# Fewer weight chunks split during attention, a new VectorE order within a period, one reciprocal for seven tiles, six warming matmuls

## The chip, the cores and the metric

The kernel runs on one core of a Trainium2 chip. The metric is the device time of one execution in microseconds (us), and less is better. The engines of the core work side by side and meet at semaphores: TensorE (PE in the profile, its weight loads PEld), VectorE (DVE), ScalarE (ACT), GpSimd (POOL) and SyncE (SP), which only issues DMAs.

## The reference

Causal attention over 24 heads (batch 2, 12 heads, 448 positions, head size 64), then two feed-forward blocks, each of two layers:

```python
scores = scale * np.matmul(q, k.transpose(0, 1, 3, 2))
scores = np.where(mask, -1000000000.0, scores)
scores = scores - np.max(scores, axis=-1, keepdims=True)
attn = np.exp(scores)
attn = attn / (np.sum(attn, axis=-1, keepdims=True) + 1e-09)
x = np.matmul(attn, v)                         # -> (896, 768)
h = x @ w_in;  g = np.maximum(h, 0.0) + alpha * np.minimum(h, 0.0);  x = g @ w_out
h = x @ w_in2; g = (h + 1)**2 / 4 between -1 and 1, h above, 0 below; out = g @ w_out2
```

The weights are drawn in 64-bit floats; the host only lays them out, and the kernel reads them as pairs of 32-bit words.

## The kernel before

**Attention.** The heads are worked in 12 pairs (`NP` = 12). A period n does the scores of pair n, the transposes of pair n-1 and the product with v of pair n-2, so three pairs are in flight. Period 0 is written apart (`first_pair`), periods 12 and 13 empty the pipeline. The program's order is the order in the code (`manual_schedule`): each engine runs its own instructions strictly one after the other.

The scores of a pair are four row blocks i = 0 to 3. Blocks 0, 1 and 2 are 128, 256 and 384 wide and have one tile for each head of the pair; block 3 is 448 wide and holds both heads in one tile. That makes seven tiles. In a period

- TensorE does `scores` of pair n (L347 for block 3, L353 for blocks 2, 1, 0), `attnv` of pair n-2 (L435), and the transposes of pair n-1 (`transp`: L407 for block 3, L415 for block 2, L425 for blocks 1 and 0).
- VectorE does `low` (L364): mask, scale and row minimum for the seven tiles. It then copies transposed tiles out of PSUM: block 3 (L511), the first tile of block 2 (L512), block 0 (L515). ScalarE copies the other tile of block 2 (L513) and block 1 (L514).
- ScalarE does `expo` (L373) on the seven tiles.
- VectorE then adds 1e-9 to the row sums and takes the reciprocal (`inverse`, L380 and L381), and GpSimd multiplies the tiles by it (L386). This is done twice in a period: first for the three tiles of blocks 3 and 2, at the period's end for the four tiles of blocks 1 and 0.
- `evac_x` brings the finished output of pair n-2 out of PSUM as a high and a low part: ScalarE rounds (`high`, L220), VectorE subtracts (`low`, L223).

Seven PSUM banks go round over the scores and the transposes (12 uses a period), the eighth holds the output of `attnv`. A tile of the next scores waits until the use of its bank seven places earlier has been read. Block 2's second tile takes the bank of the L511 copy, the tiles of block 1 those of L512 and L513, the tiles of block 0 those of L514 and L515.

**Weights.** 80 chunks of 64-bit weights are loaded, turned into a 32-bit value and split into a rounded high part and a rest, so that TensorE can multiply in its fast mode. A chunk takes: a magnitude on ScalarE (L112), `clamp` (L128), `low_bits` (L134), `high_bits` (L140), `last_bits` (L146) followed by the rounding on ScalarE (L149), and `rest` (L152). Chunks 0, 1 and 2 are prepared by the generator `prime` during attention. It is stepped once in each period from 1 on, ahead of `high`, so that one step is one or two of these operations, and clamp and rest run on GpSimd. Chunks 3 and on are split by VectorE and ScalarE while TensorE multiplies with the chunks before (`run_layer`).

**The four layers.** 2304 matmuls of 448 columns (`products`, L255). A chunk of the first layer is 36 of them. The first ones, with the first chunk, run already in periods 12 and 13 (`early_tiles`, `FILL`).

**The start.** `warm_up` issues three matmuls of 512 columns on a tile of zeros while the first inputs are loaded.

## Time and profile before

| | us |
|---|---|
| runs shown, three: lowest, median, highest | 561.75, 571.18, 571.21 |
| the profiled execution: its own time | 561.79 |
| its span, first to last instruction | 560.0 |
| attention: up to the last `attnv` and the unbroken row of layer matmuls | 92.75 |
| the four layers after that | 467.25 |

The page names each engine's busy time and share of the span. The view by stretches gives busy times between chosen moments; the timeline gives instructions in order of time, neighbours of one line merged, with the idle time ahead of them and what ended it. The two slower runs lie 1.7% above the profiled execution.

### The profile page before, as it was taken

What the parts mean: (1) busy time and instruction counts of PE and PEld (TensorE: products, weight loads), DVE (VectorE), ACT (ScalarE), POOL (GpSimd) and SP (SyncE); (2) the same over time, 40 slices, a digit from 0 to 9 for tenths busy, and PEclk for the clock granted to TensorE, in tenths of its full rate; (3) what the DMA queues carried; (4) which work ended last, traced back from release to release, by engine and by line L of the source; (5) the groups of instructions that cost most, each with busy time, mean ns of one, the idle gap of its engine ahead of it and who ended that gap; (6) DMA issues with size and microseconds to landing.
All of it is one profiled execution on the core that took longest, in us unless ns stands there. A gap on an engine that the chain in (4) does not pass through costs nothing.

```text
span 560.0 us, 8112 instructions
## 1 busy us (share of the span) xinstructions
PE 552.2 (99%) x2883; PEld 486.4 (87%) x2883; DVE 420.0 (75%) x812; ACT 236.6 (42%) x485; POOL 147.3 (26%) x170
## 2 busy tenths in 40 slices
PE   8999999999999999999999999999999999999997
PEld 4666567999999999999999999999999999999996
DVE  5888884888898988765666678898888867555740
ACT  6877772333333323332323345555554423222220
POOL 5776861333333331000000013333333300000000
PEclk9999999999999999999999999999999999999999
DMA  7543520333232224433423432333322244343421
GB/s 261 163 128 88 167 73 1 114 110 102 95 99 103 77 74 132 133 82 107 128 100 112 169 90 100 111 114 113 114 95 75 77 140 150 114 141 117 146 70 35
DMA packets 24040, 61.88 MB, mean 110 GB/s; under 512 B 3392, under 2 KB 12352, under 8 KB 24000
## 3 DMA queue, kind: packets, MB, share of 16 engines
q1 hardware_dynamic: 21984, 59.76, 33.7%
q10 hardware_dynamic: 2016, 1.61, 0.8%
q8 instruction: 23, 0.38, 0.3%
q14 instruction: 17, 0.14, 0.1%
HBM read 58.60 MB, written 2.75 MB: 110 GB/s over the span
## 4 chain that ended last, share of the span: by engine, by line
PE 86%; DVE 7%; ACT 4%; issue 1%; DMA 1%; POOL 0%; ACTq 0%; DVEq 0%; POOLq 0%
PE ps L255 83%; ACT pexp L373 3%; DVE pexp L364 2%; PE o_ps L435 1%; DVE pt L511 1%; DVE x L223 1%; ACT x L220 1%; DVE pt L512 1%; PE ps L353 1%; DMA qk_raw<-qk 1%; DVE pt L515 1%; DVE stat L380 0%; DVE w_f L146 0%; PE ps L415 0%; PE ps L407 0%
## 5 line engine op out<-in xcount | busy, mean ns | idle before, releaser
L255 PE MATMUL ps<-x,w_split 128*128 128x448 f32 x1152 | 234.5, 365 | 0.0
L255 PE MATMUL ps<-g,w_split 128*128 128x448 f32 x1152 | 233.8, 365 | 0.0
L255 PEld LDWEIGHTS ps<-g,w_split 128*128 128x128 f32 x1152 | 216.3, 188 | 17.1
L255 PEld LDWEIGHTS ps<-x,w_split 128*128 128x128 f32 x1152 | 216.1, 188 | 17.2
L184 POOL TENSOR_TENSOR g<-act_g,g 128x448 fp32r<-128x448 f32 x64 | 85.5, 1337 | 272.5 <-ACT g L183 272.4
L149 ACT CAST w_split<-w_f 128x512 fp32r<-128x512 f32 (+1 forms) x80 | 56.6, 707 | 124.7 <-DVE w_f L146 82.0
L152 DVE TENSOR_TENSOR w_split<-w_f,w_split 128x512 fp32r<-128x512 f32 (+1 forms) x77 | 63.1, 820 | 52.3 <-ACT w_split L149 52.3
L183 ACT CAST g<-act_g 128x448 fp32r<-128x448 f32 x64 | 36.2, 565 | 81.5 <-DVE act_g L196 71.6
L140 DVE SCALAR_TENSOR_TENSOR w_f<-w_raw,w_f 128x512 uint32<-128x512 uint32 (+1 forms) x80 | 63.4, 793 | 1.4
L146 DVE SCALAR_TENSOR_TENSOR w_f<-w_raw,w_f 128x512 uint32<-128x512 uint32 (+1 forms) x80 | 63.4, 793 | 1.4
L128 DVE TENSOR_SCALAR w_f<-w_f 128x512 f32<-128x512 f32 (+1 forms) x77 | 56.4, 733 | 8.7 <-ACT w_f L112 8.6
L112 ACT ACTIVATE w_f<-w_raw 128x512 f32<-128x512 f32 (+1 forms) x80 | 61.2, 765 | 0.6 <-DMA w_raw<-w 0.6
L386 POOL TENSOR_SCALAR pexp<-pexp,stat 128x256 f32<-128x256 f32 (+3 forms) x84 | 44.7, 552 | 24.4 <-DVE stat L381 14.4
L373 ACT ACTIVATE pexp<-pexp,stat 128x128 f32<-128x128 f32 (+3 forms) x84 | 43.7, 521 | 16.7 <-DVE stat L364 16.7
L134 DVE TENSOR_SCALAR w_f<-w_f 128x512 uint32<-128x512 uint32 (+1 forms) x80 | 38.4, 480 | 1.4
L208 ACT ACTIVATE act_t<-act_t,half 128x448 f32<-128x448 f32 x32 | 21.5, 671 | 37.4 <-DVE act_t L207 37.4
L364 DVE CUSTOM_DVE_ANT_0 pexp<-ps,mask 128x128 f32<-128x128 f32 (+3 forms) x84 | 32.5, 447 | 4.7 <-PE ps L353 4.3
L353 PEld LDWEIGHTS ps<-qk_raw 64*128 64x128 f32 x144 | 17.0, 196 | 15.8 <-issue 4.9
L353 PE MATMUL ps<-qk_raw 64*128 64x256 f32 (+2 forms) x144 | 25.9, 424 | 1.8 <-ACT pt L513 1.1
L233 DVE COPY o_sb<-ps 128x224 f32<-128x224 f32 x12 | 4.7, 391 | 29.9 <-ACT o_sb L233 29.9
L191 DVE TENSOR_SCALAR act_t<-ps,alpha_sb 128x448 f32<-128x448 f32 x32 | 21.8, 681 | 3.8 <-PE ps L255 3.7
L435 PE MATMUL o_ps<-pt,v 128*64 128x448 f32 (+3 forms) x192 | 23.4, 386 | 0.0
(42 smaller groups left out, 254.7 us busy)
## 6 DMA issues: line engine op xcount, KB each, us to landing
w_raw<-w SPq DMA_DIRECT2D x32, 768.0 KB, 4.3
w_raw<-w SPq DMA_DIRECT2D x48, 512.0 KB, 3.6
qk_raw<-qk SPq DMA_DIRECT2D x11, 448.0 KB, 3.8
out<-o_sb SPq DMA_DIRECT2D x12, 112.0 KB, 1.7
out<-o_sb ACTq DMA_DIRECT2D x12, 112.0 KB, 1.7
v<-v SPq DMA_DIRECT2D x12, 56.0 KB, 3.9
v<-v SPq DMA_DIRECT2D x12, 48.0 KB, 3.4
v<-v SPq DMA_DIRECT2D x12, 40.0 KB, 2.8
```

The source lines that it names most:

```text
L112: nc.scalar.activation(out=f32(w), in_=f32(hi), func=AF.Abs)
L128: side.tensor_scalar(out=f32(w), in0=f32(w), scalar1=HI_MIN, scalar2=HI_MAX, op0=ALU.max, op1=ALU.min)
L140: nc.vector.scalar_tensor_tensor(out=w, in0=hi, scalar=0xC0000000, in1=w, op0=ALU.bitwise_and, op1=ALU.bitwise_or)
L146: nc.vector.scalar_tensor_tensor(out=w, in0=lo, scalar=29, in1=w, op0=ALU.logical_shift_right, op1=ALU.bitwise_or)
L149: nc.scalar.copy(s[:, 0, :n], f32(w))
L152: side.tensor_sub(s[:, 1, :n], f32(w), f32(s[:, 0, :n]))
L184: nc.gpsimd.tensor_sub(t[:, 1, :], g, f32(t[:, 0, :]))
L255: nc.tensor.matmul(ps[b][:, :S], lhsT=ws[:, part, k * 128:(k + 1) * 128], rhs=src[b, kk][:, xp, :], start=first and part == 0 and xp == 0, ...
L353: nc.tensor.matmul(ps[j][:, :w], lhsT=t[r, 0, w - 128:w], rhs=t[r, 1, :w], start=True, stop=True)
L364: nc.vector.tensor_tensor_reduce(out=self.pexp[p][:, o:o + w], in0=b[:, :w], in1=mask3 if i == 3 else mask[:, 384 - w:], scale=-SCALE, sca ...
L373: nc.scalar.activation(out=e, in_=e, func=AF.Exp, bias=self.st[p][:, 0, n:n + 1], scale=-1.0, accum_out=self.st[p][:, 1, n:n + 1],)
L386: nc.gpsimd.tensor_scalar(out=e, in0=e, scalar1=self.st[p][:, 2, n:n + 1], scalar2=1.0, op0=ALU.mult, op1=ALU.mult)
```

## The change

- `NPRIME` is gone. `prime` now names a place for each of its steps, (period, slot): slot 0 is behind the exponentials of block 0, slot 1 at the end of the period. Chunk 0 is split in periods 1 to 4, chunk 1 at the end of period 11 and in period 12, chunk 2 in periods 12 and 13.
- `clamp` runs on VectorE always; only chunk 0's `rest` stays on GpSimd. The ScalarE steps (magnitude, rounding) come behind the period's copies.
- `inverse` is called once in a period, for all seven tiles, at its end (the first pair excepted, whose two halves stay).
- VectorE's copies of blocks 3 and 2 come ahead of `evac_x`'s `low`, which comes ahead of the copy of block 0.
- Four warming matmuls, and two more behind the first block's scores.

```diff
--- before.py
+++ after.py
@@ -41,8 +41,7 @@
 
 
     NV = 4
-    NWARM = 3
-    NPRIME = 3
+    NWARM = (4, 2)
     FILL = (2, 1)
     P0 = {3: 0, 2: S, 1: S + 768, 0: S + 1280}
     PW = S + 1536
@@ -67,9 +66,10 @@
 
         z = const.tile([128, 512], F32R, tag="zero", name="zero")
         nc.vector.memset(f32(z), 0.0)
-        for _ in range(NWARM):
+        while True:
             ps = bank()
             nc.tensor.matmul(ps, lhsT=z[:, :128], rhs=z, start=True, stop=True)
+            yield
 
     def constants():
         nc.vector.memset(half, 0.5)
@@ -112,7 +112,7 @@
             nc.scalar.activation(out=f32(w), in_=f32(hi), func=AF.Abs)
             self.n_abs += 1
 
-        def split_ops(self, side=nc.vector):
+        def split_ops(self, side=None):
 
             if self.n_split == len(self.chunks):
                 return []
@@ -125,7 +125,7 @@
 
             def clamp():
 
-                side.tensor_scalar(
+                nc.vector.tensor_scalar(
                     out=f32(w), in0=f32(w), scalar1=HI_MIN, scalar2=HI_MAX, op0=ALU.max, op1=ALU.min
                 )
 
@@ -146,32 +146,59 @@
                 nc.vector.scalar_tensor_tensor(
                     out=w, in0=lo, scalar=29, in1=w, op0=ALU.logical_shift_right, op1=ALU.bitwise_or
                 )
+                if side is None:
+                    hi_part()
+
+            def hi_part():
                 nc.scalar.copy(s[:, 0, :n], f32(w))
 
             def rest():
-                side.tensor_sub(s[:, 1, :n], f32(w), f32(s[:, 0, :n]))
-
-            return [clamp, low_bits, high_bits, last_bits, rest]
+                (side or nc.vector).tensor_sub(s[:, 1, :n], f32(w), f32(s[:, 0, :n]))
+
+            ops = [clamp, low_bits, high_bits, last_bits, hi_part, rest]
+            return ops if side else ops[:4] + ops[5:]
 
         def prime(self):
+
 
 
             self.load()
             self.load()
-            yield
+            yield 1, 1
             self.magnitude()
-            for i in range(NPRIME):
-                clamp, low, high, last, rest = self.split_ops(nc.gpsimd)
-                clamp()
-                yield
-                low()
-                yield
-                high()
-                self.magnitude()
-                yield
-                last()
-                rest()
-                self.load()
+            clamp, low, high, last, hi_part, rest = self.split_ops(nc.gpsimd)
+            yield 2, 0
+            clamp()
+            low()
+            yield 3, 0
+            high()
+            yield 4, 0
+            last()
+            yield 4, 1
+            hi_part()
+            rest()
+            self.load()
+            self.magnitude()
+            clamp, low, high, last, rest = self.split_ops()
+            yield NP - 1, 1
+            self.magnitude()
+            clamp()
+            low()
+            high()
+            last()
+            self.load()
+            yield NP, 0
+            rest()
+            clamp, low, high, last, rest = self.split_ops()
+            yield NP, 1
+            clamp()
+            low()
+            yield NP + 1, 1
+            high()
+            last()
+            self.load()
+            rest()
+            self.magnitude()
 
         def next(self):
             self.n_used += 1
@@ -375,11 +402,12 @@
                     accum_out=self.st[p][:, 1, n:n + 1],
                 )
 
-        def inverse(self, p, half):
-            st = self.st[p][:, :, :3] if half == 0 else self.st[p][:, :, 3:]
+        def inverse(self, p, tiles=(3, 2, 1, 0)):
+            lo, hi = self.place(tiles[0], 0)[2], self.place(tiles[-1], tiles[-1] != 3)[2] + 1
+            st = self.st[p][:, :, lo:hi]
             nc.vector.tensor_scalar_add(st[:, 1], st[:, 1], 1e-9)
             nc.vector.reciprocal(st[:, 2], st[:, 1])
-            for i in (3, 2) if half == 0 else (1, 0):
+            for i in tiles:
                 for j in range(1 if i == 3 else 2):
                     o, w, n = self.place(i, j)
                     e = self.pexp[p][:, o:o + w]
@@ -442,6 +470,14 @@
             return evac_x(self.o.pop(p), m, b)
 
     with tc.manual_schedule():
+        def weights(n, slot):
+            while prime and prime[0] <= (n, slot):
+                prime[0] = next(steps, (NP + 9, 0))
+
+        def step(gen, n):
+            for _ in range(n):
+                next(gen, None)
+
         wts = Weights()
         ps_s, ps_o = (
             ctx.enter_context(tc.tile_pool(name=f"ps_{n}", bufs=b, space=PSUM)) for n, b in (("s", 7), ("o", 1))
@@ -450,7 +486,8 @@
             ap = pa.enter_context(tc.tile_pool(name="attn", bufs=2))
             at = Attention(ap)
             at.load_qk(0)
-            warm_up()
+            warm = warm_up()
+            step(warm, NWARM[0])
             at.load_qk(1)
             constants()
             at.load_qk(2)
@@ -459,18 +496,17 @@
             at.clear_v()
             early = {}
             fill = early_tiles(((0, 1),))
-            prime = wts.prime()
-
-            def step(gen, n):
-                for _ in range(n):
-                    next(gen, None)
+            steps = wts.prime()
+            prime = [next(steps)]
 
             def first_pair():
-                ps = {i: at.scores(0, i) for i in (0, 1, 2, 3)}
+                ps = {0: at.scores(0, 0)}
+                step(warm, NWARM[1])
+                ps.update((i, at.scores(0, i)) for i in (1, 2, 3))
                 for i in (0, 1, 2):
                     at.low(0, i, ps[i])
                     at.expo(0, i)
-                at.inverse(0, 1)
+                at.inverse(0, (1, 0))
                 at.low(0, 3, ps[3])
                 at.expo(0, 3)
 
@@ -487,7 +523,7 @@
                     at.low(n, 3, ps[3])
                     at.expo(n, 3)
                 if n == 1:
-                    at.inverse(0, 0)
+                    at.inverse(0, (3, 2))
                 cp = {}
                 if old:
                     for i in (0, 1, 2, 3) if n == 1 else (3, 2, 1, 0):
@@ -498,23 +534,23 @@
                         at.low(n, i, ps[i])
                     at.expo(n, 2)
                     at.expo(n, 1)
-                    at.inverse(n, 0)
-                if n >= 1:
-                    step(prime, 1)
                 if out_p:
                     high()
                 if new:
                     at.expo(n, 0)
+                weights(n, 0)
+                if old:
+                    nc.vector.tensor_copy(*cp[3][0])
+                    nc.vector.tensor_copy(*cp[2][0])
                 if out_p:
                     low()
                 if old:
-                    nc.vector.tensor_copy(*cp[3][0])
-                    nc.vector.tensor_copy(*cp[2][0])
+                    nc.vector.tensor_copy(*cp[0][0])
                     nc.scalar.copy(*cp[2][1])
                     nc.scalar.copy(*cp[1][0])
-                    nc.vector.tensor_copy(*cp[0][0])
                 if new:
-                    at.inverse(n, 1)
+                    at.inverse(n)
+                weights(n, 1)
 
             for n in range(NP + 2):
                 if n == 0:
@@ -523,13 +559,11 @@
                     period(n)
                 if n + 3 < NP:
                     at.load_qk(n + 3)
-                if n == 0:
-                    step(prime, 1)
                 if n + 1 < NP:
                     at.load_v(n + 1)
             for _ in fill:
                 pass
-            for _ in prime:
+            for _ in steps:
                 pass
         gpool = ctx.enter_context(tc.tile_pool(name="g", bufs=1))
         ep = ctx.enter_context(tc.tile_pool(name="ep", bufs=2))
```

What this makes of VectorE's instructions in period 4, a period in which both programs do one step of a weight chunk; x_2 is the output of pair 2, pt the transposed tiles of pair 3, w_f the chunk's 32-bit value. Before:

```order
L364 ISA pexp,stat<-ps,mask 128x128
L364 ISA stat 128x1
L380 TENSOR_SCALAR stat<-stat 128x3
L381 RECIPROCAL stat<-stat 128x3
L146 SCALAR_TENSOR_TENSOR w_f_241<-w_raw,w_f_241 128x768
L223 TENSOR_TENSOR x_2_477<-o_ps,x_2_477 128x448
L511 COPY pt<-ps 128x4x2x64
L512 COPY pt<-ps 128x3x128
L515 COPY pt<-ps 128x2x128
L380 TENSOR_SCALAR stat<-stat 128x4
L381 RECIPROCAL stat<-stat 128x4
```

and with the change:

```order
L391 ISA pexp,stat<-ps,mask 128x128
L391 ISA stat 128x1
L146 SCALAR_TENSOR_TENSOR w_f_258<-w_raw,w_f_258 128x768
L543 COPY pt<-ps 128x4x2x64
L544 COPY pt<-ps 128x3x128
L250 TENSOR_TENSOR x_2_475<-o_ps,x_2_475 128x448
L548 COPY pt<-ps 128x2x128
L408 TENSOR_SCALAR stat<-stat 128x7
L409 RECIPROCAL stat<-stat 128x7
```

The subtraction for x_2 has moved behind two of the three copies, and the early pair of addition and reciprocal is gone.

ScalarE in the same period and the next, from the 256-wide exponentials on (x_3 is the output of pair 3). Before:

```order
L373 ACTIVATE pexp,stat<-pexp,stat 128x256 x2
L149 CAST w_split<-w_f_241 128x768
L220 CAST x_2_477<-o_ps 128x448
L373 ACTIVATE pexp,stat<-pexp,stat 128x128 x2
L513 COPY pt<-ps 128x3x128
L514 COPY pt<-ps 128x2x2x128
L373 ACTIVATE pexp,stat<-pexp,stat 128x448
```

and with the change:

```order
L400 ACTIVATE pexp,stat<-pexp,stat 128x256 x2
L247 CAST x_2_475<-o_ps 128x448
L400 ACTIVATE pexp,stat<-pexp,stat 128x128 x2
L549 COPY pt<-ps 128x3x128
L550 COPY pt<-ps 128x2x2x128
L153 CAST w_split<-w_f_258 128x768
L112 ACTIVATE w_f_533<-w_raw 128x768
L400 ACTIVATE pexp,stat<-pexp,stat 128x448
```

The chunk's rounding stood ahead of the rounding of x_2, and now stands behind both copies, with the next chunk's magnitude.

VectorE from the end of period 11 to the first steps of the layers; x_4 and x_5 are the outputs of pairs 10 and 11. Before:

```order
L515 COPY pt<-ps 128x2x128
L380 TENSOR_SCALAR stat<-stat 128x4
L381 RECIPROCAL stat<-stat 128x4
L223 TENSOR_TENSOR x_4_1210<-o_ps,x_4_1210 128x448
L511 COPY pt<-ps 128x4x2x64
L512 COPY pt<-ps 128x3x128
L515 COPY pt<-ps 128x2x128
L223 TENSOR_TENSOR x_5_1253<-o_ps,x_5_1253 128x448
L128 TENSOR_SCALAR w_f_987<-w_f_987 128x768
```

and with the change:

```order
L409 RECIPROCAL stat<-stat 128x7
L128 TENSOR_SCALAR w_f_533<-w_f_533 128x768
L134 TENSOR_SCALAR w_f_533<-w_f_533 128x768
L140 SCALAR_TENSOR_TENSOR w_f_533<-w_raw,w_f_533 128x768
L146 SCALAR_TENSOR_TENSOR w_f_533<-w_raw,w_f_533 128x768
L156 TENSOR_TENSOR w_split<-w_f_533,w_split 128x768
L543 COPY pt<-ps 128x4x2x64
L544 COPY pt<-ps 128x3x128
L250 TENSOR_TENSOR x_4_1182<-o_ps,x_4_1182 128x448
L548 COPY pt<-ps 128x2x128
L128 TENSOR_SCALAR w_f_1148<-w_f_1148 128x768
L134 TENSOR_SCALAR w_f_1148<-w_f_1148 128x768
```

Ten steps for chunks 1 and 2 now stand here, five of them between the last reciprocal and the last pair's copies (the three that are not shown follow x_5).

## Rows read from the trace of the kernel before

**Rows 1.** The page, busy us (share of the span) and instructions of each engine:
```profile
PE 552.2 (99%) x2883; PEld 486.4 (87%) x2883; DVE 420.0 (75%) x812; ACT 236.6 (42%) x485; POOL 147.3 (26%) x170
```
**Rows 2.** By stretches: edges, length, then busy us of each engine, clock, DMA:
```profile
18.07:24.41 6.34, 6.34 (x52) 4.51 (x48) 5.83 (x26) 5.01 (x18) 4.97 (x11) 1.00 0.47 133
...
81.49:87.74 6.25, 6.25 (x47) 4.93 (x45) 3.00 (x12) 3.37 (x13) 3.40 (x7) 1.00 0.00 0
87.74:92.75 5.01, 5.01 (x42) 3.81 (x38) 2.02 (x4) 1.50 (x3) 0.00 (x0) 1.00 0.01 3
92.75:560.00 467.25, 463.57 (x2290) 429.23 (x2286) 348.92 (x538) 169.55 (x274) 85.54 (x64) 1.00 0.33 106
```
**Rows 3.** Timeline of TensorE, period 9: start, length, engine, line, instruction:
```profile
62.99 0.97 PE L347 MATMUL ps<-qk_raw 64*64 64x448 f32 x4
63.89 1.57 PE L353 MATMUL ps<-qk_raw 64*128 64x384 f32 x12
65.39 1.95 PE L435 MATMUL o_ps<-pt,v 128*64 128x448 f32 x16
67.27 0.66 PE L407 MATMUL ps<-ident,pexp 128*128 128x128 f32 x4
...
68.42 0.82 PE L425 MATMUL ps<-ident,pexp 128*128 128x128 f32 x6
69.17 0.59 PE L347 MATMUL ps<-qk_raw 64*64 64x448 f32 x2
```
**Rows 4.** Timelines of VectorE, ScalarE and TensorE, a period with weight steps:
```profile
53.46 0.93 DVE L146 SCALAR_TENSOR_TENSOR w_f<-w_raw,w_f 128x768 uint32<-128x768 uint32 x1
54.42 0.83 ACT L149 CAST w_split<-w_f 128x768 fp32r<-128x768 f32 x1 [0.30 <-DVE w_f L146]
55.71 0.62 DVE L223 TENSOR_TENSOR x<-o_ps,x 128x448 fp32r<-128x448 f32 x1 [1.33 <-ACT x L220]
56.88 1.56 PE L353 MATMUL ps<-qk_raw 64*128 64x384 f32 x10 [0.38 <-ACT pt L513]
```
**Rows 5.** Timeline of VectorE, period 11, which has no weight step:
```profile
78.56 0.41 DVE L515 COPY pt<-ps 128x256 f32<-128x256 f32 x1
...
79.21 0.62 DVE L364 CUSTOM_DVE_ANT_0 pexp<-ps,mask 128x448 f32<-128x448 f32 x1
...
83.27 0.62 DVE L223 TENSOR_TENSOR x<-o_ps,x 128x448 fp32r<-128x448 f32 x1 [1.01 <-ACT x L220]
83.81 0.68 DVE L511 COPY pt<-ps 128x512 f32<-128x512 f32 x1
...
84.87 0.42 DVE L515 COPY pt<-ps 128x256 f32<-128x256 f32 x1
```
**Rows 6.** Timeline of GpSimd, multiplications of three, seven, three and four tiles:
```profile
53.73 2.28 POOL L386 TENSOR_SCALAR pexp<-pexp,stat 128x448 f32<-128x448 f32 x3 [1.37 <-ACT pexp L373]
...
60.74 3.67 POOL L386 TENSOR_SCALAR pexp<-pexp,stat 128x256 f32<-128x256 f32 x7
...
82.45 1.77 POOL L386 TENSOR_SCALAR pexp<-pexp,stat 128x448 f32<-128x448 f32 x3 [1.44 <-ACT pexp L373]
85.74 1.63 POOL L386 TENSOR_SCALAR pexp<-pexp,stat 128x256 f32<-128x256 f32 x4 [1.53 <-DVE stat L381]
```
**Rows 7.** Timeline of the start and of period 1:
```profile
1.44 1.65 PE L72 MATMUL ps<-zero 128*128 128x512 f32 x3 [1.44 <-DVE half L75]
...
4.44 2.51 PE L353 MATMUL ps<-qk_raw 64*128 64x256 f32 x8 [0.61 <-DMA qk_raw<-qk]
...
13.21 0.90 ACT L112 ACTIVATE w_f<-w_raw 128x768 f32<-128x768 f32 x1
...
14.94 0.79 DVE L380 TENSOR_SCALAR stat<-stat 128x4 f32<-128x4 f32 x1
```
**Rows 8.** Timeline of VectorE, first chunk split during the layers:
```profile
93.98 0.55 DVE L128 TENSOR_SCALAR w_f<-w_f 128x768 f32<-128x768 f32 x1
...
101.47 0.96 DVE L152 TENSOR_TENSOR w_split<-w_f,w_split 128x768 fp32r<-128x768 f32 x1 [0.42 <-ACT w_split L149]
```

## The prediction

> **What bounds the kernel now.** I read the page first: TensorE is busy for 99% of the span [rows 1], so a gain must come from matmul time that is not needed or from waits that the merged busy time hides. The stretches say where to look. From 92.75 us on, the layers take 467.25 us, with TensorE busy for 463.57 of them in about 2290 matmuls, 0.202 us each [rows 2]. The change touches none of these matmuls, so that part moves only if it is starved. Attention is what is left: 92.75 us.
>
> There a period is the distance between two first transposes (L407). Period 2 has them at 18.07, period 11 at 81.49 [rows 2]: nine periods in 63.42 us, 7.05 each. Two things could set this, and each has a row.
>
> TensorE alone: in period 9 it runs without a wait, scores of block 3 at 62.99, the other scores at 63.89, the product with v at 65.39, transposes at 67.27, the last of them at 68.42, the next scores at 69.17 [rows 3]. That is 6.18 us, and no period can be shorter with this work.
>
> The ring of the other engines: in period 11, without a weight step, it goes from the copy of block 0 (78.56) to the first `low` (79.21), over ScalarE's exponentials and the rounding of x to VectorE's subtraction (83.27, for which VectorE idled 1.01), the copies of blocks 3 and 2 (83.81), and the copy of block 0 (84.87) [rows 5]: 6.31 us, just above TensorE's 6.18. In the other two kinds of period a weight step lies in that ring: in period 7 VectorE's last step at 53.46 and ScalarE's rounding of 0.83 at 54.42 (after an idle 0.30) come ahead of the rounding of x, the subtraction comes at 55.71 after 1.33 us of idling, and TensorE's scores wait for ScalarE's copy until 56.88 [rows 4]. So attention is bound by a ring of waits, lengthened by weight steps, with TensorE 0.13 us under the shortest form of it.
>
> **The change, part by part.**
>
> *Order on VectorE.* The copies of blocks 3 and 2 (83.81 to 84.87, 1.06 us) leave the stretch behind the subtraction and use the 1.01 us in which VectorE idled [rows 5]. The ring becomes 0.65 (78.56 to 79.21) + 4.06 (79.21 to 83.27) + 0.54 (83.27 to 83.81) = 5.25 us. That is under 6.18, so TensorE becomes the bound, and the 1.06 is not all gained.
>
> *One reciprocal.* It saves one addition and one reciprocal. But the first three multiplications, which now run in the middle of a period, start only at its end. The new ring: copy of block 0 (84.87) to the first multiplication (85.74), 0.87; seven multiplications, 1.77 + 1.63 = 3.40; the last transposes, at most 0.75 (68.42 to 69.17) [rows 3, 5, 6]. Sum 5.02 us, again under 6.18. TensorE reaches the transposes only behind the scores and the product with v, and that hides the multiplications.
>
> *Weight steps.* Two of three chunks leave periods 2 to 10, and ScalarE's steps come behind its copies. With all rings below it, a free period costs TensorE's 6.18: 9 x 6.18 = 55.6 instead of 63.42, **-7.8 us**.
>
> *What chunk 0 gives back.* Its clamp, low, high and last steps run in periods 2, 3 and 4 on VectorE, now beside the seven multiplications. Rows price this: three multiplications took 2.28 beside the step L146 and 1.77 alone, so a step with two inputs costs GpSimd 0.51; a run of seven took 3.67 beside a low step against 3.40, so a step with one input costs 0.27 [rows 4, 6]. Together at most 2 x 0.27 + 2 x 0.51 = 1.56 us, and nothing if the spare 1.16 us of the GpSimd ring covers each. VectorE is late out of period 1, so I do not expect the whole cover: **+1.0** (0 to 1.6). The rounding of 0.83 and a magnitude of 0.90 on ScalarE in period 4 lie behind the copies; the spare time of ScalarE's ring (6.18 - 5.25 = 0.93) and one late start of exponentials take them. Without that cover they would cost 0.8 once.
>
> The Trainium skill (SBUF — State Buffer, section "Who interferes with whom") says that a VectorE instruction with two SBUF inputs and a GpSimd instruction that reads SBUF exclude each other for the whole instruction. The 0.51 agrees in kind: 0.66 us of overlap (53.73 to 54.39) cost 0.51. By the rule, a step that falls wholly inside the run would cost its full 0.93, and the chunk's price would be an estimated 2.4 instead of 1.0.
>
> *Period 1.* The magnitude (0.90) leaves its place ahead of the last exponentials, and GpSimd's clamp no longer lies beside the addition of 0.79 (in period 11 copy, addition and reciprocal together take 0.65, 78.56 to 79.21) [rows 5, 7]. At most 0.9; TensorE's own work behind it takes up half: **-0.4** (-0.4 to 0).
>
> *Warming.* Three matmuls take 1.65 us, 0.55 each. A fourth delays the first scores by up to 0.55, and two more do not fit the idle 0.61 ahead of the next ones: up to +0.9 together. Against it, these eight instructions take 2.51 us (from 4.44), where twelve take 1.50 in period 9 [rows 3, 7]. If the added work makes them run at that pace, up to 1.2 comes back, and more on the scores behind them. No row shows TensorE kept busy here. I take **0**, between -0.9 and +0.9.
>
> *The end of attention.* Behind the last reciprocal VectorE runs four steps of chunk 1, and a fifth ahead of the last pair's copies. I count from e, the end of period 11's transposes. Before, the next transposes came 6.25 after L407 [rows 2], which is e + 4.35 (6.25 less 69.17 - 67.27 = 1.90), and the last of them started some 1.45 later, e + 5.8. The multiplications start at about e + 1.3 (a copy at e + 0.4, then 0.87) and last 3.40, stretched by two steps at 0.27 and three at 0.51: 2.07. They end at e + 6.8; with 0.2 for the hand-over the last transposes come 1.2 late. TensorE's matmuls with chunk 0 and the last product with v are queued behind them. VectorE's copies are done near the same time. **+1.2** (0 to 2.1).
>
> *The layers.* Chunk 2's last steps fall behind x_5: high and last (0.93 each), the rounding, the rest of 0.96, so it is split some 5 us after the last product with v. TensorE needs it only after 18 matmuls of chunk 0 and 36 of chunk 1, 54 x 0.202 = 10.9. Chunk 3 was ready at 102.43 (101.47 + 0.96) and needed at about 92.75 + 90 x 0.202 = 110.9 [rows 2, 8]. It comes some 2 us later against 8.5 of spare time: 0. Each microsecond beyond that cover would cost one.
>
> **Sum**, against the profiled execution's own 561.79: -7.8 + 1.0 - 0.4 + 0 + 1.2 = -6.0, so **555.8 us**. With the bounds: -7.8 - 0.4 - 0.9 = -9.1 (552.7) to -7.8 + 1.6 + 0.9 + 2.1 = -3.2 (558.6). The median of the runs shown is 571.18, 9.4 above the profiled execution; the lowest run is the profile's twin. If the median falls at that upper level again, it reads 565.2.
>
> **The rivals.**
>
> *TensorE's 6.18 is no floor.* Some of its time between matmuls could be waits that the timeline does not name. Then a period falls to the ring of 5.25, another 9 x 0.93 = 8.4 us: 547.4. Against it: the gaps between the instructions of [rows 3] come back in many periods, whatever the others do.
>
> *The gain is given back to GpSimd.* With all seven multiplications behind one reciprocal, the last transposes wait for them. The ring of 5.02 has 1.16 to spare; if contention and hand-overs bring it to 6.7, each of nine periods costs 0.5 more, and the time is 560.3. For it: chunk 0's steps and the end do just this. Against it: a run of seven already exists, with 3.67 [rows 6], and free periods have no VectorE step beside it.
>
> *Slower.* The same ring, in every period: past 7.05 us, that is with the seven multiplications at 5.4 instead of 3.40, the periods are longer than before. At 7.9 (6.3 for the seven) the nine cost 7.7 more than before instead of 7.8 less: 571.3. For it: GpSimd now starts in one burst just as VectorE starts the next `low`. Against it: `low` and the copies read PSUM, and the rows beside them show no stretch (1.77 and 1.63) [rows 6].
>
> **How the numbers follow.** Main case 0.78, floor gone 0.06, given back to GpSimd 0.13, slower 0.03. About 2% (11 us) is what a measurement of this kernel tells from no change, since its runs spread by 1.7%. Faster by over 2%: the floor case, 0.06, and about 0.10 from the main case, where a median at the lower level is set against one at the upper level. Slower by over 2%: 0.03. The rest, 0.81, is within 2%. The range reaches from 552, the main case's lower bound, over the given-back case to 565.5, the main case at the upper level. The main case's own range is 552.7 to 558.6.
>
> **What the changed profile would show.** First transposes 6.2 us apart in periods 5 to 10; VectorE's subtraction behind two copies without an idle 1.0; in periods 2 to 4 the last transposes released by GpSimd; the unbroken row of layer matmuls from about 86.8 us instead of 92.75. I am wrong if the free periods stay near 7 us, if they fall well under 6.18, or if TensorE waits for w_split behind attention.

## The result, and the profile after

The changed kernel takes 556.31 us (median of four runs, 556.26 to 556.34), the kernel before 566.47 (median of four, 561.75 to 571.21). The ratio is 0.9903, with a 95% interval of 0.9879 to 0.9927: about 1% faster, within 2%. The forecast was 555.8 in a range of 552 to 565.5, with "within 2%" the likeliest. The profiled execution of the changed kernel took 556.29, its span is 554.5 against 560.0.

The unbroken row of layer matmuls takes 467.3 us in some traces and 476.4 in others (last section); two of the four runs of before lie 9.4 us above the other two and are left out of the ratio, and the kernels below are compared by the moment at which that row begins.

Page of the kernel after, busy us (share of the span) and instructions of each engine, to be read beside [rows 1]:
```profile
PE 548.3 (99%) x2886; PEld 484.1 (87%) x2886; DVE 421.0 (76%) x795; ACT 236.2 (43%) x485; POOL 135.5 (24%) x165
```
Stretches of the kernel after: edges, length, then busy us of each engine (instructions), granted clock, DMA. The edges are the first transposes of periods 4 and 11 (L435 now) and the start of the unbroken row:
```profile
31.27:74.49 43.22, 43.22 (x340) 28.42 (x337) 36.28 (x141) 36.50 (x124) 26.23 (x51) 1.00 0.38 110
74.49:87.23 12.74, 11.83 (x87) 8.93 (x83) 10.06 (x17) 5.43 (x14) 6.26 (x9) 1.00 0.18 63
87.23:554.50 467.27, 463.56 (x2289) 429.34 (x2286) 351.39 (x541) 171.19 (x276) 85.51 (x64) 1.00 0.35 108
```
TensorE stays at 99%, and its share says as little as before. The stretches tell it all. Nine periods, 18.70 to 74.49, take 55.79 us where they took 63.42: the last seven 43.22, or 6.17 each, all of it TensorE busy. The end of attention takes 12.74 where it took 6.25 + 5.01 = 11.26, and TensorE is idle there for 0.9. The layers take 467.27 against 467.25 [rows 2].

| us | predicted | measured |
|---|---|---|
| start: up to the first transposes of period 2 (18.07, now 18.70) | -0.4 | +0.63 |
| nine periods (63.42, now 55.79) | -7.8 + 1.0 = -6.8 | -7.63 |
| end of attention (11.26, now 12.74) | +1.2 | +1.48 |
| layers | 0 | +0.02 |
| sum | -6.0 | -5.50 |

A free period of the kernel after, timeline of TensorE (start, length, engine, line, instruction):
```profile
45.52 0.97 PE L374 MATMUL ps<-qk_raw 64*64 64x448 f32 x4
46.42 1.57 PE L380 MATMUL ps<-qk_raw 64*128 64x384 f32 x12
47.92 1.95 PE L463 MATMUL o_ps<-pt,v 128*64 128x448 f32 x16
49.80 0.66 PE L435 MATMUL ps<-ident,pexp 128*128 128x128 f32 x4
...
51.69 0.97 PE L374 MATMUL ps<-qk_raw 64*64 64x448 f32 x4
```
and the other engines in the same period, with the idle time ahead and what ended it:
```profile
46.84 3.36 POOL L414 TENSOR_SCALAR pexp<-pexp,stat 128x448 f32<-128x448 f32 x7 [2.81 <-DVE stat L409]
...
50.49 0.69 DVE L543 COPY pt<-ps 128x512 f32<-128x512 f32 x1 [0.97 <-PE ps L435]
51.56 0.61 DVE L250 TENSOR_TENSOR x<-o_ps,x 128x448 fp32r<-128x448 f32 x1
...
53.49 0.67 ACT L400 ACTIVATE pexp<-pexp,stat 128x448 f32<-128x448 f32 x1 [1.19 <-DVE stat L391]
```
The distance 45.52 to 51.69 is the 6.17 of [rows 3], 6.18, but now it comes in every free period. VectorE idles 0.97 us waiting for TensorE's transposes, GpSimd 2.81 and ScalarE 1.19: now they wait, not TensorE. The subtraction at 51.56 starts without an idle; before, it came after 1.01 to 1.33 us of it [rows 4, 5].

### The profile page after: what moved, and what is told of

Read it like the earlier page. It is cut to its first block, busy times and chain, and to the rows that moved or that the text cites. A ratio compares the mean times of both kernels' runs of the same rounds, so it can differ in the third digit from the quotient of the medians.

```text
span 554.5 us, 8090 instructions
## 1 busy us (share of the span) xinstructions
PE 548.3 (99%) x2886; PEld 484.1 (87%) x2886; DVE 421.0 (76%) x795; ACT 236.2 (43%) x485; POOL 135.5 (24%) x165
## 4 chain that ended last, share of the span: by engine, by line
PE 84%; POOL 1%; DVE 0%; ACT 0%; issue 0%; ACTq 0%
PE ps L282 84%; POOL pexp L414 1%; PE o_ps L463 0%; DVE o_sb L260 0%; ACT o_sb L260 0%; PE ps L453 0%; ACTq L260 0%
## 5 line engine op out<-in xcount | busy, mean ns | idle before, releaser
L156 DVE TENSOR_TENSOR w_split<-w_f,w_split 128x512 fp32r<-128x512 f32 (+1 forms) x79 | 65.2, 825 | 53.8 <-ACT w_split L153 53.8
L128 DVE TENSOR_SCALAR w_f<-w_f 128x512 f32<-128x512 f32 (+1 forms) x80 | 58.4, 730 | 9.0 <-ACT w_f L112 8.8
L380 PEld LDWEIGHTS ps<-qk_raw 64*128 64x128 f32 x144 | 13.5, 197 | 12.7 <-DVE stat L408 4.9
L463 PEld LDWEIGHTS o_ps<-pt,v 128*64 128x64 f32 x192 | 12.9, 136 | 10.9 <-issue 5.9
L234 DVE TENSOR_SCALAR act_t<-ps 128x448 f32<-128x448 f32 x32 | 19.9, 621 | 3.0 <-PE ps L282 2.4
```

Source lines behind the costliest of these rows:

```text
L128: nc.vector.tensor_scalar(out=f32(w), in0=f32(w), scalar1=HI_MIN, scalar2=HI_MAX, op0=ALU.max, op1=ALU.min)
L156: (side or nc.vector).tensor_sub(s[:, 1, :n], f32(w), f32(s[:, 0, :n]))
L463: nc.tensor.matmul(ps[j * D:(j + 1) * D, c * 128:S], lhsT=t[:, c, j, :], rhs=pt[:, j, c * 448:c * 320 + S], start=c == 0, stop=c == NQ - 1,)
```

## The experiments

Theory A is the prediction's account with the measured sizes: before, a ring of waits through ScalarE and VectorE set the period; after, TensorE's own 6.18 us sets it; it takes both the new order and the moved weight steps to get there, and the loss at the end comes from chunk 1's steps. The quantities compared are "2 to 11" (first transposes of period 2 to those of period 11), "end" (from there to the unbroken row) and the moment at which the unbroken row begins. Apart from before, after and the last three kernels, each of these was run once. old_steps (568.88 us), spread (563.91) and pad_te (567.65) missed the spans that were expected of them, because their layers took 476.4 us; that says nothing about their attention.

| kernel | period 2's transposes | 2 to 11 | end | row begins |
|---|---|---|---|---|
| before | 18.07 | 63.42 | 11.26 | 92.75 |
| after | 18.70 | 55.79 | 12.74 | 87.23 |
| old_order | 18.71 | 56.72 | 13.82 | 89.25 |
| old_steps | 18.29 | 61.21 | 11.22 | 90.72 |
| two_inverses | 17.83 | 55.56 | 12.17 | 85.56 |
| spread | 18.71 | 55.82 | 11.21 | 85.74 |
| warm_3 | 18.16 | 55.79 | 12.74 | 86.69 |
| warm_0 | 17.91 | 55.79 | 12.74 | 86.44 |
| pad_te | 18.11 | 58.63 | 12.74 | 89.48 |
| pad_te_before | 18.38 | 63.03 | 11.26 | 92.67 |
| pad_ve | 17.77 | 55.82 | 12.74 | 86.33 |
| both_warm_6 | 18.69 | 57.48 | 11.21 | 87.38 |
| both_warm_3 | 18.08 | 57.47 | 11.22 | 86.77 |
| both_warm_0 | 17.37 | 57.48 | 11.22 | 86.07 |

### What bounds a period: pad_te, pad_te_before, pad_ve

Two more matmuls on zeros, in periods 5 to 10, ahead of block 3's scores, in the kernel after and in the one before.

```diff
             if i == 3:
                 ps = bank()
+                for _ in range(2 * (5 <= p <= 10)):
+                    nc.tensor.matmul(ps, lhsT=zero[0][:, :128], rhs=zero[0], start=True, stop=True)
```

> The changed kernel with work added: ahead of the scores of block 3 in periods 5 to 10 TensorE does two more matmuls of 512 columns on zeros, which the scores overwrite. At full pace each takes about 0.2 us. Theory A (TensorE sets the free periods): each of the six periods grows by the whole 0.44 us, the span by about 2.6, to 557.1. Rival B (another engine's ring sets them): the span stays within 0.5 us of 554.5.

> The kernel before with the same added work: two more matmuls of 512 columns on zeros ahead of the scores of block 3 in periods 5 to 10, about 0.44 us a period. Theory A (a ring of waits through VectorE and ScalarE sets the periods of the kernel before, and TensorE waits 0.6 to 1.3 us in most of them): periods of 7 us and more do not grow, those of 6.3 by up to 0.3, and the span by less than 1.0 us, to 560.0 to 561.0. Rival B (TensorE is the bound there too): the span grows by the whole 2.6.

Timeline of TensorE in pad_te, first transposes of two periods with the added matmuls between them:
```profile
37.35 0.66 PE L439 MATMUL ps<-ident,pexp 128*128 128x128 f32 x4
...
39.07 0.71 PE L375 MATMUL ps<-zero 128*128 128x512 f32 x2
...
43.99 0.66 PE L439 MATMUL ps<-ident,pexp 128*128 128x128 f32 x4
```
The period is 43.99 - 37.35 = 6.64 us, 0.47 more than 6.17, and 6.64 to 6.65 in all six padded periods. In the kernel before, the same matmuls cost nothing: from period 4's transposes to period 11's (81.49 in [rows 2]) it takes 49.93 us without them and 49.88 with them. Timelines of TensorE in before, then in pad_te_before:
```profile
31.56 0.66 PE L407 MATMUL ps<-ident,pexp 128*128 128x128 f32 x4
```
```profile
31.53 0.66 PE L411 MATMUL ps<-ident,pexp 128*128 128x128 f32 x4
...
81.41 0.66 PE L411 MATMUL ps<-ident,pexp 128*128 128x128 f32 x4
```
So TensorE bounds the periods after the change and did not before.

pad_ve puts two memsets, 0.96 us of VectorE's time, ahead of VectorE's copies in periods 5 to 10 of the kernel after:

```diff
                 weights(n, 0)
+                for _ in range(2 * (5 <= n <= 10)):
+                    nc.vector.memset(scratch, 0.0)
                 if old:
```

> The changed kernel with work added on VectorE: behind the row minima in periods 5 to 10, two memsets of 128x512 on a scratch tile, about 0.48 us each, 0.96 a period. Theory A (TensorE sets the free periods and VectorE idles 0.97 us just there): the periods stay at 6.17 to 6.25 us, and the span grows by less than 0.5. Rival B (VectorE is as near the bound as TensorE): each period grows by half the added work or more, the span by 2.9 or more.

It costs nothing: 2 to 11 takes 55.82, and the free periods stay at 6.17. So the spare time of about 0.93 us that the prediction's ring of 5.25 leaves under TensorE's 6.18 is there.

### Which part of the change brings it: old_order, old_steps

old_order keeps the moved weight steps and the one reciprocal, and puts the subtraction back ahead of the copies:

```diff
                 weights(n, 0)
+                if out_p:
+                    low()
                 if old:
                     nc.vector.tensor_copy(*cp[3][0])
                     nc.vector.tensor_copy(*cp[2][0])
-                if out_p:
-                    low()
-                if old:
```

> The changed kernel with one part undone: VectorE does the subtraction for x ahead of the copies of blocks 3 and 2 again, as before the change. Theory A (free periods are bound by TensorE at 6.17 us, and the order only takes 1.06 us out of a ring that would be 6.31 us): periods 5 to 10 become 6.3 us instead of 6.17, the span grows by 9 x 0.13 = 1.2 us, to about 555.7. Rival B (the order on VectorE is what gained): the periods go back towards 7 us, and the span to about 560 or more.

Timelines of VectorE (period 11's subtraction) and TensorE (the last transposes) in old_order:
```profile
77.20 0.62 DVE L250 TENSOR_TENSOR x<-o_ps,x 128x448 fp32r<-128x448 f32 x1 [1.36 <-ACT x L247]
...
85.64 0.33 PE L453 MATMUL ps<-ident,pexp 128*128 128x128 f32 x1 [0.71 <-POOL pexp L414]
```
The last four periods are 6.31 to 6.32 us, the ring that [rows 5] gave, with VectorE idle 1.36 ahead of the subtraction, as in period 11; the two behind chunk 0's steps are still 6.18 and 6.24. What was not expected is the end, 13.82 against 12.74: in period 11 this wait stands ahead of the copies and of the seven tiles' reciprocal, which starts 3.90 us after that period's first transposes instead of 2.82, and the multiplications, chunk 1's steps and the last transposes come 1.1 later with it.

old_steps does the opposite: the new order and the one reciprocal, but the weight steps as before, one in each period, with clamp and rest on GpSimd:

```diff
-            prime = [next(steps)]
+            prime = []
...
+                if n >= 1:
+                    step(steps, 1)
                 if out_p:
                     high()
```

(With `prime` empty, the calls of `weights` do nothing; `clamp` and `rest` are given to GpSimd again in lines that are not shown.)

> The changed kernel with the weight steps back in their old places: three chunks in periods 1 to 10, one step a period ahead of ScalarE's rounding of x, clamp and rest on GpSimd. The new order on VectorE, the one reciprocal and the warming stay. Theory A (the ring is 5.25 us, a step on ScalarE adds 0.93, which TensorE's 6.17 still hides; but clamp 2.77 and rest 1.81 on GpSimd beside 3.4 of multiplications exceed 6.17 by about 1.8 us in three periods): the span grows by about 5 us, to 559 to 561, almost all of it in the periods in which GpSimd has clamp and rest, and the other periods stay near 6.2 to 6.4. Rival B (the weight steps in the ring set the period whatever the order): every period with a ScalarE step goes to 7 us or more, and the span to 562 or more.

Timelines of GpSimd and TensorE in old_steps:
```profile
33.25 1.82 POOL L153 TENSOR_TENSOR w_split<-w_f,w_split 128x768 fp32r<-128x768 f32 x1 [0.37 <-ACT w_split L150]
35.16 2.77 POOL L129 TENSOR_SCALAR w_f<-w_f 128x768 f32<-128x768 f32 x1
38.02 3.73 POOL L388 TENSOR_SCALAR pexp<-pexp,stat 128x448 f32<-128x448 f32 x7
39.08 0.89 PE L409 MATMUL ps<-ident,pexp 128*128 128x128 f32 x4 [1.14 <-POOL pexp L388]
```
Two of every three periods take 7.2 to 7.4 us, the third 6.17: 61.21 in all, 5.4 more than after and near the 5 us that theory A put there, but in two periods of three instead of one. GpSimd has 1.82 + 2.77 us of weight steps ahead of 3.73 of multiplications, and TensorE's transposes wait 1.14 for it; the last transposes of the same pair, already in the next period, take 1.48 instead of 0.82, so one late run of multiplications lengthens two periods. The gain is given back to GpSimd here, as in the prediction's rival, though by weight steps on GpSimd and not by contention. So of the 7.63 us, the order and the one reciprocal bring 2.21 without the moved steps (63.42 - 61.21), and the moved steps bring 6.70 with one reciprocal but the old order (63.42 - 56.72).

### One reciprocal or two: two_inverses

```diff
                     at.expo(n, 1)
+                    at.inverse(n, (3, 2))
...
-                    at.inverse(n)
+                    at.inverse(n, (1, 0))
```

> The changed kernel with two additions and reciprocals a period again: for blocks 3 and 2 behind their exponentials, for blocks 1 and 0 at the period's end. Theory A (in free periods VectorE has 0.97 us of idle time, so the second pair costs nothing; behind the last reciprocal of period 11 three of seven multiplications are done before chunk 1's steps start, so the last transposes are released about 1 us earlier): free periods stay at 6.17 us, and the span falls by 0.5 to 1.2 us, to 553.3 to 554.0. Rival B (the one reciprocal is part of the gain): free periods grow by 0.3 us, and the span to 556 or more.

Timeline of GpSimd at the end of attention in two_inverses:
```profile
73.60 1.77 POOL L414 TENSOR_SCALAR pexp<-pexp,stat 128x448 f32<-128x448 f32 x3 [1.58 <-PE o_ps L463]
76.56 3.47 POOL L414 TENSOR_SCALAR pexp<-pexp,stat 128x256 f32<-128x256 f32 x4 [1.19 <-DVE stat L409]
```
The free periods are as theory A said. All nine periods are 6.17 to 6.18, and the end is 12.17 instead of 12.74, since three multiplications are done ahead of chunk 1's steps. The one reciprocal loses 0.23 in periods 2 and 3 and 0.57 at the end, and gains nothing in free periods. The unbroken row begins 1.67 earlier than in the kernel after; 0.87 of that is a start that came out quicker with the same code (17.83 against 18.70).

### The end of attention: spread

All three chunks are split as the change splits chunk 0, from periods 2, 5 and 8 on, and none at the end:

```diff
+            for p in (2, 5, 8):
+                clamp, low, high, last, hi_part, rest = self.split_ops(nc.gpsimd)
+                yield p, 0
+                clamp()
+                low()
+                yield p + 1, 0
+                high()
+                yield p + 2, 0
+                last()
+                yield p + 2, 1
+                hi_part()
+                rest()
+                self.load()
+                self.magnitude()
```

> The changed kernel with chunks 1 and 2 split in the same way as chunk 0, in periods 5 to 7 and 8 to 10, instead of behind the last reciprocal. Theory A (the 1.48 us that the end of attention lost come from chunk 1's five VectorE steps beside the last seven multiplications; a chunk in the middle costs 0.22): the distance from the first transposes of period 11 to the unbroken layer matmuls goes from 12.74 back to about 11.3, periods 5 to 10 gain 0.4 us together, and the span falls by about 1.0, to 553.5. Rival B (the end lost its time to the one reciprocal, chunk 1 or not): the distance stays near 12.7, and the span grows by the 0.4, to 554.9.

Timelines of GpSimd and TensorE at the end of attention in spread:
```profile
77.75 3.38 POOL L395 TENSOR_SCALAR pexp<-pexp,stat 128x448 f32<-128x448 f32 x7 [1.00 <-DVE stat L390]
...
83.86 1.95 PE L444 MATMUL o_ps<-pt,v 128*64 128x448 f32 x16
```
The end is 11.21, 1.53 less than after and the same as before. The multiplications take 3.38 instead of 5.85. The periods with the steps of chunks 1 and 2 cost nothing (6.17 from period 4 on). So the whole loss at the end comes from the weight steps that the change put there, and the free periods had room for them. spread moves chunk 2's steps away too; that chunk 1's are the ones that cost is read from the timeline of the kernel after, where chunk 2's first step starts at 85.17, behind the last multiplication and the last transposes.

### Both improvements together: both_warm_6, both_warm_3, both_warm_0

These have the edits of spread and of two_inverses, with 6, 3 and no warming matmuls.

> The changed kernel with two parts altered that cost time: chunks 1 and 2 split in periods 5 to 10 as chunk 0 is (1.53 us less at the end of attention when done alone), and two additions and reciprocals a period (0.23 us less in periods 2 and 3 when done alone). The six warming matmuls stay. Theory A (the two gains stand beside each other, the start aside): the nine periods take 9 x 6.17 = 55.5 us, the end 11.2, and the time is 1.5 to 1.8 us below the changed kernel's 556.3: 554.5 to 554.8. Rival B (both remove the same wait at the end): 0.3 us or less beyond what one of them brings, and the nine periods stay at 55.8.

> The kernel with both parts altered, and the three warming matmuls of before instead of six. Theory A (the three added ones cost the 0.8 to 0.9 us by which the scores of block 1 start later, and what they give back by an earlier rise of TensorE's pace comes in some executions only): the median is 0.3 to 0.9 us below the same kernel with six, 553.7 to 554.3. Rival B (the earlier rise pays for the added matmuls on the whole): the median is the same as with six or above.

> The kernel with both parts altered, and no warming matmul. Theory A (warming gives nothing: the second scores wait for their data until 4.2 to 4.5 us, whatever stands ahead of them): the same as with three within 0.3 us, 553.6 to 554.3. Rival B (warming brings the rise of TensorE's pace forward): 0.5 us or more above the one with three.

The gains don't add, and neither theory of both_warm_6 holds. 2 to 11 takes 57.5 in all three, 1.9 more than in two_inverses: two periods (5 to 6 and 8 to 9) take 7.12 to 7.14, the others 6.17. The first of them in both_warm_6, timelines of ScalarE, VectorE and TensorE:
```profile
34.33 0.84 ACT L153 CAST w_split<-w_f 128x768 fp32r<-128x768 f32 x1
35.06 0.94 ACT L112 ACTIVATE w_f<-w_raw 128x768 f32<-128x768 f32 x1
...
37.88 0.61 DVE L389 TENSOR_SCALAR stat<-stat 128x3 f32<-128x3 f32 x1 [0.36 <-ACT pexp L381]
...
39.18 0.88 DVE L134 TENSOR_SCALAR w_f<-w_f 128x768 uint32<-128x768 uint32 x1
39.98 0.67 DVE L525 COPY pt<-ps 128x512 f32<-128x512 f32 x1
...
40.00 2.52 PE L361 MATMUL ps<-qk_raw 64*128 64x384 f32 x12
```
and the same place in spread:
```profile
38.28 0.67 DVE L524 COPY pt<-ps 128x512 f32<-128x512 f32 x1
...
40.28 1.57 PE L361 MATMUL ps<-qk_raw 64*128 64x384 f32 x12
```
ScalarE's rounding and magnitude hold up its exponentials. The early addition on VectorE needs three of them, and it stands ahead of the next chunk's clamp and low steps and of the copies. So the copies come at 39.98 instead of 38.28, and TensorE's twelve scores take 2.52 instead of 1.57 because they wait for the banks of these copies. In two_inverses no clamp follows in the next period, in spread no addition waits. This is read from the timelines, no run was made for it alone. The three kernels begin the unbroken row at 87.38, 86.77 and 86.07, later than spread (85.74) and two_inverses (85.56); their medians over four runs are 565.44, 564.77 and 564.35, against 562.23 for the kernel before on the same chip. In all three traces the layers take 476.4 us, so these times don't tell how the kernels would compare at equal layers. No version was shown in repeated runs to be quicker than the changed kernel; the lowest single times are 554.59 (two_inverses) and 555.47 (warm_0).

### The warming matmuls: warm_3, warm_0

In the kernel after, `NWARM` is set to `(3, 0)` and `(0, 0)` instead of `(4, 2)`.

> The changed kernel with the three warming matmuls of before, and none behind the first block's scores. Theory A (the three added ones only delay the first scores, since the eight score instructions behind them take 2.51 us with or without them): the first transposes of period 2 come 1.0 us earlier, at 17.7, and the span falls by 1.0, to 553.5. Rival B (the added matmuls also shorten something behind them): the span stays within 0.3 us of 554.5 or grows.

> The changed kernel with no warming matmul at all. Theory A (warming at the start has no effect on the scores behind it, whose pace is set later): the first scores start with their data at 3.03 us as with three, and the span is that of the kernel with three, about 553.5. Rival B (the three warming matmuls do raise TensorE's pace earlier): the scores and transposes of periods 0 and 1 run at the slow pace for longer, and the span is 1 us or more above that with three.

TensorE's start in the kernel after:
```profile
4.18 1.22 PE L71 MATMUL ps<-zero 128*128 128x512 f32 x2
5.33 2.51 PE L380 MATMUL ps<-qk_raw 64*128 64x256 f32 x8
7.76 2.75 PE L374 MATMUL ps<-qk_raw 64*64 64x448 f32 x8
...
13.89 0.60 PE L435 MATMUL ps<-ident,pexp 128*128 128x128 f32 x4
```
and in warm_0:
```profile
4.20 2.51 PE L380 MATMUL ps<-qk_raw 64*128 64x256 f32 x8 [0.40 <-DMA qk_raw<-qk]
6.64 3.12 PE L374 MATMUL ps<-qk_raw 64*64 64x448 f32 x8
```
and in two_inverses, whose start is the code of the kernel after:
```profile
5.33 2.16 PE L380 MATMUL ps<-qk_raw 64*128 64x256 f32 x8
7.42 1.72 PE L374 MATMUL ps<-qk_raw 64*64 64x448 f32 x8
```
With six warming matmuls the eight scores behind them start at 5.33 in all eight traces, with three (before and pad_te_before among them) at 4.32 to 4.71, with none at 4.20 and 4.25. That delay is sure. What it buys comes in some executions only. With three or none the eight scores take 2.50 or 2.51 us in all six traces. With six they take the same in after, old_order, spread and both_warm_6, but 2.10 to 2.44 in old_steps, pad_te, two_inverses and pad_ve, and there block 3's scores take 1.72 where the other traces have 2.21 to 3.12. In these four TensorE reached its quicker pace sooner than in the other four, and period 1's first transposes come at 12.96 to 13.30 instead of 13.88 to 13.90; with three they come at 12.88 to 13.35, with none at 12.56 and 13.11.

Period 2's transposes come at 17.91 without warming, 18.16 with three and 18.70 with six, and in the three kernels of the last part at 17.37, 18.08 and 18.69. That looks like an order, but the seven traces with six warming matmuls and the same code up to period 1 spread over 17.77 to 18.71, which takes in both with three. So one run each of warm_3 and warm_0 decides neither theory. The repeated runs of the last part say a little more: the median with three lies 0.67 us below the one with six, as theory A of both_warm_3 said, and the lowest runs 0.59 (556.04 and 556.63). None against three is 0.42 lower, which neither theory of both_warm_0 said, with ranges that overlap (564.22 to 565.01 and 556.04 to 565.04). Three instead of six looks a little better there; that none is better still is not shown.

## Why the prediction was right, point by point

**What bounds the kernel: right.** The ring before, TensorE after. pad_te and pad_te_before show it from both sides, and the last periods of old_order give the 6.31 us of the ring.

**-7.8 for the free periods: right.** Seven periods stand at 6.17. TensorE's 6.18 is a floor (pad_te), so the rival of 547.4 falls.

**+1.0 that chunk 0 gives back: mis-sized, it is 0.2.** Periods 2 to 4 take 6.35 and 6.22 and then 6.17: 0.18 + 0.05. The stretch itself is there. Timelines of GpSimd, VectorE and TensorE in periods 2 and 3:
```profile
16.50 3.96 POOL L414 TENSOR_SCALAR pexp<-pexp,stat 128x448 f32<-128x448 f32 x7 [3.05 <-DVE stat L409]
...
18.81 0.77 DVE L128 TENSOR_SCALAR w_f<-w_f 128x768 f32<-128x768 f32 x1
19.84 0.99 PE L453 MATMUL ps<-ident,pexp 128*128 128x128 f32 x6
...
22.63 4.06 POOL L414 TENSOR_SCALAR pexp<-pexp,stat 128x448 f32<-128x448 f32 x7 [2.17 <-DVE stat L409]
```
The seven multiplications take 3.96 instead of 3.36 beside two steps with one input: 0.60, near the 2 x 0.27 of the working. Beside one step with two inputs they take 4.06 and 4.05 (periods 3 and 4), 0.70 and 0.69 where the working had 0.51 from a partial overlap. So chunk 0 costs GpSimd 1.99 us, more than the 1.56 called the most and less than the other estimate, 2.4. What was mis-sized is the cover: the 1.16 us that GpSimd's ring has to spare hid nearly all of it, and only the last transposes of these two periods take longer, 0.99 and 0.88 us instead of 0.82. VectorE's lateness out of period 1 is there (the multiplications start 2.2 us ahead of the transposes in period 2 and 2.96 in a free period), and it fits that it costs the 0.2: in spread the same steps in later periods cost nothing.

**Period 1, -0.4: right.** From period 1's first transposes to period 2's it is 18.07 - 12.90 = 5.17 before and 18.70 - 13.89 = 4.81 after. With the weight steps back in their old places (old_steps) it is 18.29 - 13.14 = 5.15, so it is the moved steps that bring it.

**Warming, 0 between -0.9 and +0.9: the term that was furthest off.** In the profiled execution period 1's transposes come 0.99 later (12.90 to 13.89), just past the bound. The delay is the size that was priced, 0.89: the eight scores start at 5.33 instead of 4.44 (the terms named, 0.55 + 1.10 - 0.61, add up to 1.04 and not 0.9). The pace that was to come back did not in this execution: the eight scores take 2.51 as before. In four other traces with the same six warming matmuls it did come in part, and there the first transposes of period 1 are 0.1 to 0.4 later than in before. So the mechanism is half right, and which half a run shows is settled by the execution; what settles it stays open.

**The end of attention, +1.2: right, a little small at 1.48.** Timelines of VectorE, GpSimd and TensorE from period 11's reciprocal on, kernel after:
```profile
77.43 0.51 DVE L128 TENSOR_SCALAR w_f<-w_f 128x768 f32<-128x768 f32 x1
77.71 5.85 POOL L414 TENSOR_SCALAR pexp<-pexp,stat 128x448 f32<-128x448 f32 x7 [2.81 <-DVE stat L409]
77.98 0.88 DVE L134 TENSOR_SCALAR w_f<-w_f 128x768 uint32<-128x768 uint32 x1
78.90 1.21 DVE L140 SCALAR_TENSOR_TENSOR w_f<-w_raw,w_f 128x768 uint32<-128x768 uint32 x1
80.14 1.23 DVE L146 SCALAR_TENSOR_TENSOR w_f<-w_raw,w_f 128x768 uint32<-128x768 uint32 x1
82.27 1.05 DVE L156 TENSOR_TENSOR w_split<-w_f,w_split 128x768 fp32r<-128x768 f32 x1 [0.90 <-ACT w_split L153]
83.61 0.33 PE L453 MATMUL ps<-ident,pexp 128*128 128x128 f32 x1 [0.72 <-POOL pexp L414]
...
85.35 1.95 PE L463 MATMUL o_ps<-pt,v 128*64 128x448 f32 x16 [0.19 <-issue]
```
The chain is the one worked out: steps beside the multiplications, these stretched by 5.85 - 3.36 = 2.49 (2.07 was said), the last transposes waiting for GpSimd, the product with v behind them.

**The layers, 0: right.** Chunk 2's last step, timeline of VectorE, ends 5.0 us into the layers (91.29 + 0.96 - 87.23), where the forecast needed it at 10.9:
```profile
91.29 0.96 DVE L156 TENSOR_TENSOR w_split<-w_f,w_split 128x768 fp32r<-128x768 f32 x1 [0.90 <-ACT w_split L153]
```

**The sum.** It is within 0.5 us partly by luck: two misses of opposite sign nearly cancel, chunk 0 costing 0.8 less than said and the start about 1.0 more, and the end adds 0.3. In an execution with the quicker start it would have come out lower. The rival "given back to GpSimd" did not come in the changed kernel, where the seven multiplications take 3.36 us in the free periods. old_steps shows that GpSimd does set the period once its weight steps come back.

## What to carry to other kernels

Where an engine is busy for 99% of the span, measure its period against the sum of its own instructions, and against the ring of waits around it: whichever is longer is the bound, and once the ring is shorter, nothing more is gained by shortening it. Work moved out of a loop to its end is not free there: put where the last results of the pipeline are still being made, one chunk's steps cost 1.5 us, while in the loop's spare time they cost nothing that the period shows. Two improvements that cost nothing alone can spend the same spare time; run them together before adding their gains.

## What the runs showed of the hardware

**Two paces of the same matmuls.** The unbroken row of layer matmuls ran at one of two paces in every trace, at a granted clock of 1.00 (2.4 GHz) both times. TensorE's layer matmuls in the kernel after and in spread, grouped by line and form (count, busy us, mean ns of one):
```profile
L282 PE MATMUL ps<-g,w_split 128*128 128x448 f32 x1152 | 233.8, 365 | 0.0
```
```profile
L263 PE MATMUL ps<-g,w_split 128*128 128x448 f32 x1152 | 238.4, 368 | 0.0
```
The layers take 467.3 us at the one and 476.4 at the other, 2% apart, and TensorE has no idle time in either. From start to start a matmul takes 0.2027 us on average or 0.2067; the rows part within the first few matmuls and keep their pace to the end. The slower one came in the traces of spread, old_steps, pad_te and the three both kernels. It does not belong to an execution as a whole: in before, old_order and pad_te_before the first twelve layer matmuls, in period 12, ran at the slower pace (0.207) and the unbroken row at the quicker. What chooses it stays open. It is also why spread, whose row begins 1.5 us earlier than after's, takes 563.91.

**TensorE's pace at the start.** Up to about 7 to 10 us its matmuls take about twice as long as later (block 3's eight scores in 3.12 us in warm_0 and in 1.72 in two_inverses, where the pace had risen before them), while the clock column of the stretches reads 1.00 throughout. The moment of the change differs between executions of the same code: about 7.0 us in two_inverses and pad_ve, 9.7 to 10 in after and spread.

**VectorE and GpSimd stretch each other.** Beside the seven multiplications at the end the weight steps with two inputs took 1.21 and 1.23 us, where chunk 2's, with GpSimd idle, took 0.95 and 0.96; the multiplications went from 3.36 to 5.85. One step with two inputs wholly inside a run of seven cost GpSimd 0.69 to 0.70 in the kernel after and took 1.09 to 1.11 itself.
